# Four column tiles for the K and V matmuls of a low-rank attention decode kernel, with K loaded first

## The chip, the cores and the metric

The kernel runs on one core of a Trainium2 chip. The metric is the device time of one execution in microseconds. Of the kernel before, single runs lie between 656.4 and 669.9 us, so medians and ratios of several runs are compared. Profiles are single executions, and their "span" is up to 6 us shorter than the time of the same run.

## The reference

```python
B, H, Sq, Skv, Dh, R = 2, 16, 1, 8192, 256, 8     # bf16, k and v are 134 MB each
kp = einsum("rn,bhnd->bhrd", e_proj, k)            # 8192 keys are projected to 8
vp = einsum("rn,bhnd->bhrd", f_proj, v)
scores = einsum("bhqd,bhrd->bhqr", q, kp) * Dh ** -0.5
o = einsum("bhqr,bhrd->bhqd", softmax(scores), vp)
```

All of k and v, 268 MB, must be read once. Everything else is small.

## The kernel before

Two heads ("a pair") are handled together in each of 16 iterations. `kt` and `vt` hold a pair's K and V, 8 MB each (64 KB in each partition), and **each has one buffer**. The 8192 keys of a head lie on 64 partitions with 128 columns `j`, so a K group is 64 matmuls of 128x512 and a V group 128 matmuls of 128x256. The stationary operand has only 32 columns in both. V's weights are softmax(scores) times `f_proj`, so V's matmuls give the output rows directly.

```python
FIRST_K = (64, 64); LAST_K = (64, 32, 16, 8, 8); LAST_V = (64, 24, 16, 10, 6, 4, 2, 2)
W_AHEAD = 24
# ... SyncE: loads
nc.sync.dma_start(out=st[:, 0], in_=e_v).then_inc(s_st, 16)      # the projections
nc.sync.dma_start(out=st[:, 1], in_=f_v).then_inc(s_st, 16)
for a in range(NP):                                               # 16 pairs
    if a > 0:
        nc.sync.wait_ge(s_kr, a)            # K's buffer is released by its last matmul
    ...                                     # load kt: whole, or in FIRST_K / LAST_K pieces
    if a > 0:
        nc.sync.wait_ge(s_vr, a)            # V's buffer likewise
    ...                                     # load vt: whole, or in LAST_V pieces
# ... TensorE, one iteration
for j in range(0, J, 2):                    # J = 128
    mm = nc.tensor.matmul(acc_k[:], lhsT=wk[:, j:j + 2, :]..., rhs=kt[:, j:j + 2, :]...,
                          start=(j == 0), stop=(j == J - 2))
mm.then_inc(s_kr, 1)
...                                         # softmax on VectorE and ScalarE
for j in range(J):
    mm = nc.tensor.matmul(o_ps[:], lhsT=wp[:, j, :], rhs=vt[:, j, :], start=False,
                          stop=(j == J - 1), skip_group_check=True)
mm.then_inc(s_vr, 1)
```

(Cuts are marked by `...`; the `wait_ge` on the landing of a load ahead of each group is left out.)

## Time and profile before

| | before |
|---|---|
| median of 3 runs (lowest to highest) | 665.48 us (660.8 to 669.93) |
| profiled run: time, span, granted TensorE clock | 656.35 us, 654.3 us, 0.896 |
| end of the last packet of a load, by the packet records | 640.6 us |

First, lines of the page of the kernel before. "q1" is the queue of the loads; its last number is the share of 16 engines' span that packets were in flight. PE is TensorE, PEld its weight loads, DVE VectorE, ACT ScalarE, POOL GpSimd, and SP SyncE. The granted clock is the share of TensorE's full clock that the throttle let through. Part 5 lines end with busy us, mean ns, then the idle time before the group and who ended it.

```profile
span 654.3 us, 7393 instructions
...
PE 522.7 (80%) x3233; PEld 327.6 (50%) x3233; DVE 98.7 (15%) x280; ACT 16.3 (2%) x36; POOL 8.3 (1%) x12
...
q1 hardware_dynamic: 6720, 268.73, 96.5%
...
HBM read 268.71 MB, written 0.02 MB: 411 GB/s over the span
...
DMA 55%; PE 43%; DVE 1%; issue 1%; SPq 0%; ACT 0%; DVEq 0%; ACTq 0%
...
L213 PE MATMUL o_ps<-vt,wp 128*32 128x256 bf16 x2048 | 258.9, 295 | 40.4 <-DMA vt<-in_v_dram 33.8
L197 PE MATMUL acc_k<-kt,wk 128*32 128x512 bf16 x1024 | 246.0, 405 | 40.7 <-DMA kt<-in_k_dram 40.7
```

TensorE waits 41 us in 14 K groups and 34 us in the V groups, 2 to 3 us each. The next fence is the view of DMA issues of the same kernel: median us from the issue of a whole 8 MB load to its landing.

```profile
vt<-in_v_dram SPq DMA_DIRECT2D x15, 23.6
kt<-in_k_dram SPq DMA_DIRECT2D x14, 24.0
```

A load that is queued in good time lands about 19.4 us after the one before it (see the changed kernel below), so here a load is issued only about 4 us before the load ahead of it has landed. I call this time the **lead**: from the issue of a load to the landing of the one before it.

The end of the execution, from the timeline of TensorE (start us, us, engine, line, operation):

```profile
617.43 13.99 PE L197 MATMUL acc_k<-kt,wk 128*32 128x512 bf16 x64
633.33 0.28 PE L203 MATMUL pb<-p_77,ones_81 1*64 1x8 f32 x4 [1.91 <-ACT p_77 L232]
635.26 15.80 PE L213 MATMUL o_ps<-vt,wp 128*32 128x256 bf16 x128 [1.65 <-DVE wp L279]
```

And in windows (from and to, length, then busy us and instructions of PE, weight loads, DVE, ACT and POOL, then granted clock, DMA share and GB/s), first the steady state, then the tail:

```profile
100.00:600.00 500.00, 404.56 (x2455) 249.42 (x2452) 73.19 (x214) 10.27 (x26) 0.00 (x0) 0.89 0.99 420
```

```profile
620.00:639.00 19.00, 15.44 (x77) 7.87 (x76) 5.83 (x17) 0.21 (x1) 0.00 (x0) 0.91 0.98 412
640.00:651.00 11.00, 11.00 (x102) 9.59 (x99) 0.00 (x0) 0.00 (x0) 0.00 (x0) 1.00 0.01 3
```

After 640 us the DMA is done and TensorE works alone for 11 us. Look also at the steady state: the DMA is "99% busy" at 420 GB/s. That share counts a packet as busy however long it takes. Most packets carry 64 KB and take 2.418 us in the median; sixteen engines at that pace would move 434 GB/s.

Where I quote idle engines and slow packets below, they are my sums over the trace's packet records: *idle* is the time in which fewer than 16 packets were in flight, weighted by the engines that had none and divided by 16; *slow* is the time of 64 KB packets above 2.418 us, divided by 16. Both are then microseconds of the whole DMA.

### The profile page before, as it was taken

Reading aid. Unit: us, or ns where it says so; the run is one execution under the profiler, and the core shown is the slowest. Engines: PE = TensorE matmul, PEld = TensorE weight load, DVE = VectorE, ACT = ScalarE, POOL = GpSimd, SP = SyncE. Lnnn points to the kernel's source line nnn. Section 1 sums busy time; section 2 is a strip of 40 time slices with the busy share of each in tenths; the row PEclk is TensorE's granted clock in tenths of the full one; section 3 lists DMA queues with packets and bytes.
Section 4 is the critical chain, followed back from the end, with each engine's and each line's share of the span. In section 5 each row is a group of like instructions: output and inputs, shape, how many; then the busy total and the mean of one; then the engine's idle time right before and its main releaser. Section 6 shows DMA issues by size and latency. Waiting matters only on the chain.

```text
span 654.3 us, 7393 instructions
## 1 busy us (share of the span) xinstructions
PE 522.7 (80%) x3233; PEld 327.6 (50%) x3233; DVE 98.7 (15%) x280; ACT 16.3 (2%) x36; POOL 8.3 (1%) x12
## 2 busy tenths in 40 slices
PE   4577988777977869868788787769877789687978
PEld 3246374453835528345363644638354373553736
DVE  1030020301103030030300203021030300303030
ACT  0200000000000000000000000000000000000000
POOL 5000000000000000000000000000000000000000
PEclk9689878899877898878999788999887898788999
DMA  9999999999999999999999999999999999999991
GB/s 367 420 437 445 409 437 389 445 437 401 425 421 437 381 445 393 441 389 389 449 449 421 413 445 417 421 449 441 421 421 421 413 433 393 449 393 409 423 414 39
DMA packets 6721, 268.75 MB, mean 411 GB/s; under 512 B 768, under 2 KB 1344, under 8 KB 1984
## 3 DMA queue, kind: packets, MB, share of 16 engines
q1 hardware_dynamic: 6720, 268.73, 96.5%
q8 instruction: 1, 0.02, 0.0%
HBM read 268.71 MB, written 0.02 MB: 411 GB/s over the span
## 4 chain that ended last, share of the span: by engine, by line
DMA 55%; PE 43%; DVE 1%; issue 1%; SPq 0%; ACT 0%; DVEq 0%; ACTq 0%
DMA kt<-in_k_dram 44%; PE acc_k L197 33%; PE o_ps L213 10%; DMA vt<-in_v_dram 7%; DMA q_69<-in_q_dram 3%; DVE prod L256 0%; PE q_ps L187 0%; SPq L137 0%; DVE wtmp L272 0%; DVE wp_83 L276 0%; PE pb L203 0%; ACT o_sb L235 0%; DVE wp L279 0%; ACT p_77 L232 0%; SPq L141 0%
## 5 line engine op out<-in xcount | busy, mean ns | idle before, releaser
L213 PE MATMUL o_ps<-vt,wp 128*32 128x256 bf16 x2048 | 258.9, 295 | 40.4 <-DMA vt<-in_v_dram 33.8
L197 PE MATMUL acc_k<-kt,wk 128*32 128x512 bf16 x1024 | 246.0, 405 | 40.7 <-DMA kt<-in_k_dram 40.7
L213 PEld LDWEIGHTS o_ps<-vt,wp 128*32 128x32 bf16 x2048 | 213.7, 105 | 82.5 <-DMA vt<-in_v_dram 40.0
L197 PEld LDWEIGHTS acc_k<-kt,wk 128*32 128x32 bf16 x1024 | 103.4, 102 | 179.9 <-DMA kt<-in_k_dram 44.6
L256 DVE SCALAR_TENSOR_TENSOR prod<-acc_k,q_sb 32x512 f32<-32x512 f32 x16 | 10.8, 678 | 288.7 <-PE acc_k L197 288.7
L253 DVE MEMSET wp<- x16 | 4.4, 272 | 215.5 <-PE o_ps L213 213.0
L203 PE MATMUL pb<-p_77,ones_81 1*64 1x8 f32 x64 | 4.5, 208 | 30.6 <-ACT p_77 L232 30.6
L272 DVE TENSOR_TENSOR wtmp<-fw,pb 128x192 f32<-128x192 bf16 (+1 forms) x32 | 22.0, 687 | 10.6 <-PE pb L203 10.1
L203 PEld LDWEIGHTS pb<-p_77,ones_81 1*64 1x64 f32 x64 | 3.1, 129 | 38.5 <-ACT p_77 L232 38.5
L276 DVE TENSOR_REDUCE wp_83<-wtmp 128x24 f32<-128x192 f32 (+1 forms) x32 | 22.0, 686 | 1.1
L230 ACT CAST q_sb<-q_ps 32x512 bf16<-32x512 f32 x16 | 9.2, 575 | 297.2 <-PE q_ps L187 297.2
L169 PE MATMUL ps_e<-st,sel 128*128 128x128 bf16 x32 | 6.9, 270 | 9.4 <-POOL sel_q L117 8.4
L232 ACT ACTIVATE p_77<-s_75 1x16 f32<-1x16 f32 x16 | 3.4, 215 | 303.1 <-DVE s_75 L268 303.1
L278 DVE CAST wp<-wp_83 64x24 f32 (+1 forms) x32 | 9.6, 299 | 4.4
L187 PE MATMUL q_ps<-q_69,sel_q 32*32 32x256 bf16 x32 | 6.4, 281 | 4.8 <-DMA q_69<-in_q_dram 4.8
L279 DVE CAST wp<-wp_83 64x24 f32 (+1 forms) x32 | 9.7, 304 | 0.4
L169 PEld LDWEIGHTS ps_e<-st,sel 128*128 x32 | 3.5, 109 | 11.3 <-issue 10.8
L169 PE MATMUL ps_f<-st,sel 128*128 128x128 bf16 x32 | 6.7, 272 | 0.0
L187 PEld LDWEIGHTS q_ps<-q_69,sel_q 32*32 x32 | 1.8, 89 | 8.3 <-issue 8.2
L169 PEld LDWEIGHTS ps_f<-st,sel 128*128 x32 | 3.8, 119 | 0.1
L110 POOL MEMSET sel<- 128x4096 bf16 x1 | 3.5, 3512 | 0.5 <-SPq L98 0.5
L260 DVE STREAM_TRANSPOSE sc_out<-sc_in 32x32 f32<-32x32 f32 x16 | 3.2, 199 | 0.5
(27 smaller groups left out, 27.6 us busy)
## 6 DMA issues: line engine op xcount, KB each, us to landing
kt<-in_k_dram SPq DMA_DIRECT2D x3, 4096.0 KB, 14.1
vt<-in_v_dram SPq DMA_DIRECT2D x1, 4096.0 KB, 13.8
kt<-in_k_dram SPq DMA_DIRECT2D x1, 2048.0 KB, 18.7
vt<-in_v_dram SPq DMA_DIRECT2D x1, 1536.0 KB, 17.1
kt<-in_k_dram SPq DMA_DIRECT2D x1, 1024.0 KB, 20.7
kt<-in_k_dram SPq DMA_DIRECT2D x2, 512.0 KB, 22.1
vt<-in_v_dram SPq DMA_DIRECT2D x1, 1024.0 KB, 19.1
vt<-in_v_dram SPq DMA_DIRECT2D x1, 640.0 KB, 20.2
```

The lines of the kernel that those rows point to most:

```text
L169: mm = nc.tensor.matmul(ps[:, bass.ds(r, 1), :].rearrange("p o j -> p (o j)"), lhsT=pick, rhs=st[:, i, x, :], start=(x == 0), stop=(x == X ...
L187: mm = nc.tensor.matmul(q_ps[:, b * Dh:(b + 1) * Dh], lhsT=sel_q[:, bass.ds(it, 1), b, :].rearrange("k a m -> k (a m)"), rhs=q16[:], start ...
L197: mm = nc.tensor.matmul(acc_k[:], lhsT=wk[:, j:j + 2, :].rearrange("p j m -> p (j m)"), rhs=kt[:, j:j + 2, :].rearrange("p j d -> p (j d)" ...
L203: mm = nc.tensor.matmul(pb[g * PH:(g + 1) * PH, :], lhsT=ones1[:], rhs=p16[:, g, :], start=True, stop=True)
L213: mm = nc.tensor.matmul(o_ps[:], lhsT=wp[:, j, :], rhs=vt[:, j, :], start=False, stop=(j == J - 1), skip_group_check=True)
L230: nc.scalar.copy(out=q_sb[:], in_=q_ps[:]).then_inc(s_qa, 1)
L253: nc.vector.memset(wp[:, :, bass.ds(old, G)], 0.0)
L256: then(0, nc.vector.scalar_tensor_tensor(out=prod[:], in0=acc_k[:], scalar=scale, in1=q_sb[:], op0=ALU.mult, op1=ALU.mult, accum_out=sc_in ...
L272: then(4 + i, nc.vector.tensor_tensor(out=wtmp[:, lo:hi], in0=fw[:, lo:hi], in1=pb[:].unsqueeze(1).to_broadcast([P, hi - lo, R]), op=ALU.m ...
L276: then(6 + i, nc.vector.reduce_sum(out=wp32[:, lo:hi], in_=wtmp[:, lo:hi], axis=AX.X))
L278: nc.vector.tensor_copy(out=wp[0:PH, lo:hi, bass.ds(col, 1)], in_=wp32[0:PH, lo:hi].unsqueeze(2))
L279: then(0, nc.vector.tensor_copy(out=wp[PH:P, lo:hi, bass.ds(col + 1, 1)], in_=wp32[PH:P, lo:hi].unsqueeze(2)), (s_wa, s_wb)[i])
```

## The change

The intent: the stationary operand has 32 columns, so three quarters of the TensorE array stand idle. K's matmuls go round four column tiles (four sets of 32 output partitions), and so do V's first 96; V's four partial sums are added by an fp32 matmul with a selection matrix (`fsel`) half way through the last 32 columns, which use two tiles, one for each half of the 256 output columns. The softmax is done on all 128 partitions at once, loads are whole 8 MB transfers except for V's last, and K's first load is issued ahead of the projections.

```diff
-FIRST_K = (64, 64)
-LAST_K = (64, 32, 16, 8, 8)
-LAST_V = (64, 24, 16, 10, 6, 4, 2, 2)
-W_AHEAD = 24
+LAST_V = (64, 32, 16, 10, 4, 2)
+SPREAD = 96
+FOLD = 112
 ...
-        nc.sync.dma_start(out=st[:, 0], in_=e_v).then_inc(s_st, 16)
-        nc.sync.dma_start(out=st[:, 1], in_=f_v).then_inc(s_st, 16)
         for a in range(NP):
             if a > 0:
                 nc.sync.wait_ge(s_kr, a)
+            nc.sync.dma_start(out=kt[:], in_=k_t[a]).then_inc(s_kd, 16)
             if a == 0:
-                load(kt, k_t[a], FIRST_K, s_kf)
+                nc.sync.dma_start(out=st[:, 0], in_=e_v).then_inc(s_st, 16)
+                nc.sync.dma_start(out=st[:, 1], in_=f_v).then_inc(s_st, 16)
 ...
-            for j in range(0, J, 2):
-                mm = nc.tensor.matmul(acc_k[:], ..., start=(j == 0), stop=(j == J - 2))
+            for i in range(J // 2):
+                mm = nc.tensor.matmul(tile4(acc_k, i % CT), ...,
+                                      start=(i < CT), stop=(i >= J // 2 - CT), skip_group_check=True)
             mm.then_inc(s_kr, 1)
 ...
             for j in range(J):
-                mm = nc.tensor.matmul(o_ps[:], lhsT=wp[:, j, :], rhs=vt[:, j, :], ...)
+                if j == FOLD:
+                    nc.tensor.wait_ge(s_ev, t1)
+                    for x in range(X):
+                        nc.tensor.matmul(tile4(o_x, x)[:, 0:DX], lhsT=fsel[:], rhs=o4_sb[:, x * DX:(x + 1) * DX], ...)
+                if j < SPREAD:
+                    mm = nc.tensor.matmul(tile4(o_4, j % CT)[:, 0:Dh], lhsT=wp[:, j, :], rhs=vt[:, j, :],
+                                          start=(j < CT), stop=(j >= SPREAD - CT), skip_group_check=True)
+                else:
+                    for x in range(X):
+                        mm = nc.tensor.matmul(tile4(o_x, x)[:, 0:DX], lhsT=wp[:, j, :],
+                                              rhs=vt[:, j, x * DX:(x + 1) * DX], ...)
             mm.then_inc(s_vr, 1)
```

(Cut: waits, semaphores, the constants, the loads of the later pairs, and the softmax, which sums by one fp32 matmul with a mask in place of a transpose. With `W_AHEAD` goes the early start of V: its matmuls began when the weights of the first 24 columns were ready, and now wait for all of them.)

More of the change, by code (lines that the diff above doesn't have):

```diff
@@ L46 @@
     GR = G * R
+    CT = 4
+    W = P // CT
+    X = 2
+    DX = Dh // X
     C = P // R
     XB = PH // C
-    assert Sq == 1 and BH == 32 and J == 128 and 2 * GR == 32 and C * XB == PH
-    assert sum(FIRST_K) == J and sum(LAST_K) == J and sum(LAST_V) == J
+    assert Sq == 1 and BH == W and J == 128 and 2 * GR == W and C * XB == PH
+    assert sum(LAST_V) == J and SPREAD % CT == 0
     scale = float(Dh) ** -0.5
-    TQ = 32
     sb = ctx.enter_context(tc.tile_pool(name="sb", bufs=1))
@@ L65 @@
     q16 = sb.tile([BH, Dh], BF16, name="q16")
-    sel_q = sb.tile([BH, NP, 2, GR * 2], BF16, name="sel_q")
-    q_sb = sb.tile([2 * GR, 2 * Dh], BF16, name="q_sb")
-    prod = sb.tile([2 * GR, 2 * Dh], FP32, name="prod")
-    sc_in = sb.tile([TQ, TQ], FP32, name="sc_in")
-    sc_out = sb.tile([TQ, TQ], FP32, name="sc_out")
-    s16 = sb.tile([1, G, R], FP32, name="s16")
-    nmax = sb.tile([1, G], FP32, name="nmax")
-    p16 = sb.tile([1, G, R], FP32, name="p16")
-    ssum = sb.tile([1, G], FP32, name="ssum")
-    rs_in = sb.tile([TQ, TQ], FP32, name="rs_in")
-    rs_out = sb.tile([TQ, TQ], FP32, name="rs_out")
-    ones1 = sb.tile([1, PH], FP32, name="ones1")
+    sel_q = sb.tile([BH, NP, 2, CT, 2, GR], BF16, name="sel_q")
+    q_sb = sb.tile([P, 2 * Dh], BF16, name="q_sb")
+    ident = sb.tile([P, P], FP32, name="ident")
+    sel_r = sb.tile([P, R], FP32, name="sel_r")
+    sel_g = sb.tile([P, G], FP32, name="sel_g")
+    gmask = sb.tile([P, G, PH], FP32, name="gmask")
+    fsel = sb.tile([P, W], FP32, name="fsel")
+    prod = sb.tile([P, 2 * Dh], FP32, name="prod")
+    sc = sb.tile([P, 1], FP32, name="sc")
+    scr = sb.tile([P, R], FP32, name="scr")
+    nmax = sb.tile([P, 1], FP32, name="nmax")
+    p32 = sb.tile([P, R], FP32, name="p32")
+    ssum = sb.tile([P, 1], FP32, name="ssum")
+    rs = sb.tile([P, 1], FP32, name="rs")
     wtmp = sb.tile([P, J, R], FP32, name="wtmp")
     wp32 = sb.tile([P, J], FP32, name="wp32")
+    o4_sb = sb.tile([P, Dh], FP32, name="o4_sb")
     o_sb = sb.tile([BH, Dh], BF16, name="o_sb")
@@ L83 @@
     ps_f = pp.tile([P, R, J], FP32, name="ps_f")
-    acc_k = pp.tile([2 * GR, 2 * Dh], FP32, name="acc_k")
-    o_ps = pp.tile([BH, Dh], FP32, name="o_ps")
-    q_ps = pp.tile([2 * GR, 2 * Dh], FP32, name="q_ps")
-    pb = pp.tile([P, R], FP32, name="pb")
+    acc_k = pp.tile([P, 2 * Dh], FP32, name="acc_k")
+    o_4 = pp.tile([P, 2 * Dh], FP32, name="o_4")
+    o_x = pp.tile([P, 4 * DX], FP32, name="o_x")
+    q_ps = pp.tile([P, 2 * Dh], FP32, name="q_ps")
+    s_ps = ps_e[:].rearrange("p r j -> p (r j)")[:, 0:R]
     k_t = k.rearrange("b h (p j) d -> (b h p) j d", p=PH).rearrange("(a q) j d -> a q j d", q=P)
@@ L94 @@
     f_v = f_proj.rearrange("r (c x j) -> (r c) x j", c=C, x=XB)
-    starts = lambda parts: {sum(parts[:i]): i for i in range(len(parts))}
+    last_v = {sum(LAST_V[:i]): i for i in range(len(LAST_V))}
     with tc.tile_critical(name="main"):
@@ L100 @@
         s_st, s_qd, s_out, s_kd, s_vd, s_kr, s_vr = (sem(n) for n in ("st", "qd", "out", "kd", "vd", "kr", "vr"))
-        s_kf = [sem(f"kf{i}") for i in range(len(FIRST_K))]
-        s_kl = [sem(f"kl{i}") for i in range(len(LAST_K))]
         s_vl = [sem(f"vl{i}") for i in range(len(LAST_V))]
-        s_zi, s_cst, s_wk, s_e, s_f, s_w0, s_f0 = (sem(n) for n in ("zi", "cst", "wk", "e", "f", "w0", "f0"))
-        s_q, s_qa, s_x, s_ex, s_pb, s_wa, s_wb = (sem(n) for n in ("q", "qa", "x", "ex", "pb", "wa", "wb"))
-        s_d = [sem(f"d{i}") for i in range(9)]
-        s_rs, s_fin = sem("rs"), sem("fin")
+        s_zi, s_id, s_cst, s_wk, s_e, s_f, s_w0, s_f0 = (
+            sem(n) for n in ("zi", "id", "cst", "wk", "e", "f", "w0", "f0"))
+        s_q, s_qa, s_sc, s_sp, s_mx, s_ex, s_w, s_o4, s_ev, s_fin = (
+            sem(n) for n in ("q", "qa", "sc", "sp", "mx", "ex", "w", "o4", "ev", "fin"))
+        s_d = [sem(f"d{i}") for i in range(8)]
         nc.gpsimd.memset(sel[:], 0.0).then_inc(s_zi, 1)
-        nc.gpsimd.wait_ge(s_zi, 1)
+        nc.gpsimd.memset(sel_q[:], 0.0).then_inc(s_zi, 1)
+        nc.gpsimd.memset(ident[:], 0.0).then_inc(s_zi, 1)
+        nc.gpsimd.wait_ge(s_zi, 3)
         for x in range(XB):
@@ L116 @@
             ).then_inc(s_zi, 1)
-        nc.gpsimd.memset(sel_q[:], 0.0).then_inc(s_zi, 1)
-        nc.gpsimd.wait_ge(s_zi, 2 + XB)
+        nc.gpsimd.affine_select(
+            out=ident[:], in_=ident[:], compare_op=ALU.not_equal, fill=1.0,
+            base=0, pattern=[[-1, P]], channel_multiplier=1,
+        ).then_inc(s_id, 1)
         for b in range(2):
-            nc.gpsimd.affine_select(
-                out=sel_q[:, :, b, b * GR:(b + 1) * GR], in_=sel_q[:, :, b, b * GR:(b + 1) * GR],
-                compare_op=ALU.not_equal, fill=1.0,
-                base=0, pattern=[[-G, NP], [-1, G], [0, R]], channel_multiplier=1,
-            ).then_inc(s_cst, 1)
+            for c in range(CT):
+                sl = sel_q[:, :, b, c, b].rearrange("k a (g r) -> k a g r", g=G)
+                nc.gpsimd.affine_select(
+                    out=sl, in_=sl, compare_op=ALU.not_equal, fill=1.0,
+                    base=0, pattern=[[-G, NP], [-1, G], [0, R]], channel_multiplier=1,
+                ).then_inc(s_cst, 1)
@@ L125 @@
         nc.vector.memset(wk[:], 0.0).then_inc(s_wk, 1)
-        nc.vector.memset(wp[:], 0.0).then_inc(s_cst, 1)
         nc.vector.memset(z0[:], 0.0)
-        nc.vector.memset(sc_in[:], 0.0)
-        nc.vector.memset(rs_in[:], 0.0)
-        nc.vector.memset(ones1[:], 1.0).then_inc(s_cst, 1)
-        NCST = 4
-        def load(dst, src, parts, sems):
-            j0 = 0
-            for js, s in zip(parts, sems, strict=True):
-                nc.sync.dma_start(out=dst[:, j0:j0 + js, :], in_=src[:, j0:j0 + js, :]).then_inc(s, 16)
-                j0 += js
@@ L140 @@
-        nc.sync.dma_start(out=st[:, 0], in_=e_v).then_inc(s_st, 16)
-        nc.sync.dma_start(out=st[:, 1], in_=f_v).then_inc(s_st, 16)
+        nc.vector.memset(wp[:], 0.0)
+        nc.vector.wait_ge(s_id, 1)
+        nc.vector.reduce_sum(out=sel_r[:], in_=ident[:].rearrange("k (i r) -> k r i", r=R), axis=AX.X)
+        nc.vector.reduce_sum(out=sel_g[:], in_=ident[:].rearrange("k (i g r) -> k g i r", g=G, r=R),
+                             axis=AX.XY).then_inc(s_id, 1)
+        nc.vector.reduce_sum(out=fsel[:], in_=ident[:].rearrange("k (c m) -> k m c", c=CT), axis=AX.X)
@@ L142 @@
+        nc.vector.wait_ge(s_id, 2)
+        nc.vector.tensor_copy(out=gmask[:],
+                              in_=sel_g[:].unsqueeze(2).to_broadcast([P, G, PH])).then_inc(s_cst, 1)
+        NCST = 2 * CT + 1
         for a in range(NP):
@@ L144 @@
                 nc.sync.wait_ge(s_kr, a)
+            nc.sync.dma_start(out=kt[:], in_=k_t[a]).then_inc(s_kd, 16)
             if a == 0:
-                load(kt, k_t[a], FIRST_K, s_kf)
+                nc.sync.dma_start(out=st[:, 0], in_=e_v).then_inc(s_st, 16)
+                nc.sync.dma_start(out=st[:, 1], in_=f_v).then_inc(s_st, 16)
                 nc.sync.dma_start(out=q16[:], in_=q_v).then_inc(s_qd, 16)
-            elif a < NP - 1:
-                load(kt, k_t[a], (J,), (s_kd,))
-            else:
-                load(kt, k_t[a], LAST_K, s_kl)
             if a > 0:
@@ L154, with tile4 @@
             if a < NP - 1:
-                load(vt, v_t[a], (J,), (s_vd,))
+                nc.sync.dma_start(out=vt[:], in_=v_t[a]).then_inc(s_vd, 16)
             else:
-                load(vt, v_t[a], LAST_V, s_vl)
-        nc.sync.wait_ge(s_fin, 1)
+                j0 = 0
+                for js, s in zip(LAST_V, s_vl, strict=True):
+                    nc.sync.dma_start(out=vt[:, j0:j0 + js], in_=v_t[a][:, j0:j0 + js]).then_inc(s, 16)
+                    j0 += js
+        nc.sync.wait_ge(s_fin, X)
         nc.sync.dma_start(out=o_v, in_=o_sb[:]).then_inc(s_out, 16)
         nc.sync.wait_ge(s_out, 16)
-        nc.tensor.wait_ge(s_zi, 2 + XB)
+        def tile4(ps, c):
+            return ps[c * W:(c + 1) * W]
+        nc.tensor.wait_ge(s_zi, 3 + XB)
         nc.tensor.wait_ge(s_st, 32)
@@ L174 @@
         nc.tensor.wait_ge(s_w0, 2)
-        nc.tensor.matmul(o_ps[:], lhsT=z0[:],
-                         rhs=wk[:, 0:Dh // GR, :].rearrange("p j m -> p (j m)"), start=True, stop=False,
-                         skip_group_check=True)
+        for x in range(X):
+            nc.tensor.matmul(tile4(o_x, x)[:, 0:DX], lhsT=z0[:],
+                             rhs=wk[:, 0:DX // GR, :].rearrange("p j m -> p (j m)"), start=True, stop=False,
+                             skip_group_check=True)
         nc.tensor.wait_ge(s_qd, 16)
-        first_k, last_k, last_v = starts(FIRST_K), starts(LAST_K), starts(LAST_V)
         with nc.tensor.Fori(0, NP) as it:
@@ L183 @@
             last = nc.tensor.snap((it // (NP - 1)) * 16)
+            tk = nc.tensor.snap((it + 1) * 16)
             tv = nc.tensor.snap((it + 1) * 16 - last)
-            tk = nc.tensor.snap(it * 16 - last)
             for b in range(2):
                 mm = nc.tensor.matmul(q_ps[:, b * Dh:(b + 1) * Dh],
-                                      lhsT=sel_q[:, bass.ds(it, 1), b, :].rearrange("k a m -> k (a m)"), rhs=q16[:],
-                                      start=True, stop=True)
+                                      lhsT=sel_q[:, bass.ds(it, 1), b].rearrange("k a c b m -> k (a c b m)"),
+                                      rhs=q16[:], start=True, stop=True)
@@ L190 @@
             mm.then_inc(s_q, 1)
             nc.tensor.wait_ge(s_kd, tk)
-            for j in range(0, J, 2):
-                if j in first_k:
-                    nc.tensor.wait_ge(s_kf[first_k[j]], 16)
-                if j in last_k:
-                    nc.tensor.wait_ge(s_kl[last_k[j]], last)
-                mm = nc.tensor.matmul(acc_k[:], lhsT=wk[:, j:j + 2, :].rearrange("p j m -> p (j m)"),
-                                      rhs=kt[:, j:j + 2, :].rearrange("p j d -> p (j d)"),
-                                      start=(j == 0), stop=(j == J - 2))
@@ L200 @@
-            mm.then_inc(s_kr, 1)
-            nc.tensor.wait_ge(s_ex, t1)
-            for g in range(G):
-                mm = nc.tensor.matmul(pb[g * PH:(g + 1) * PH, :], lhsT=ones1[:], rhs=p16[:, g, :],
-                                      start=True, stop=True)
-            mm.then_inc(s_pb, 1)
-            nc.tensor.wait_ge(s_wa, t1)
+            for i in range(J // 2):
+                mm = nc.tensor.matmul(tile4(acc_k, i % CT), lhsT=wk[:, 2 * i:2 * i + 2].rearrange("p j m -> p (j m)"),
+                                      rhs=kt[:, 2 * i:2 * i + 2].rearrange("p j d -> p (j d)"),
+                                      start=(i < CT), stop=(i >= J // 2 - CT), skip_group_check=True)
@@ L207 @@
+            mm.then_inc(s_kr, 1)
+            nc.tensor.wait_ge(s_sc, t1)
+            nc.tensor.matmul(s_ps, lhsT=gmask[:].rearrange("k g p -> k (g p)"), rhs=scr[:],
+                             start=True, stop=True).then_inc(s_sp, 1)
+            nc.tensor.wait_ge(s_w, t1)
             nc.tensor.wait_ge(s_vd, tv)
             for j in range(J):
-                if j == W_AHEAD:
-                    nc.tensor.wait_ge(s_wb, t1)
                 if j in last_v:
                     nc.tensor.wait_ge(s_vl[last_v[j]], last)
-                mm = nc.tensor.matmul(o_ps[:], lhsT=wp[:, j, :], rhs=vt[:, j, :], start=False,
-                                      stop=(j == J - 1), skip_group_check=True)
+                if j == FOLD:
+                    nc.tensor.wait_ge(s_ev, t1)
+                    for x in range(X):
+                        nc.tensor.matmul(tile4(o_x, x)[:, 0:DX], lhsT=fsel[:], rhs=o4_sb[:, x * DX:(x + 1) * DX],
+                                         start=False, stop=False, skip_group_check=True)
+                if j < SPREAD:
+                    mm = nc.tensor.matmul(tile4(o_4, j % CT)[:, 0:Dh], lhsT=wp[:, j, :], rhs=vt[:, j, :],
+                                          start=(j < CT), stop=(j >= SPREAD - CT), skip_group_check=True)
+                    if j == SPREAD - 1:
+                        mm.then_inc(s_o4, 1)
+                else:
+                    for x in range(X):
+                        mm = nc.tensor.matmul(tile4(o_x, x)[:, 0:DX], lhsT=wp[:, j, :],
+                                              rhs=vt[:, j, x * DX:(x + 1) * DX], start=False,
+                                              stop=(j == J - 1), skip_group_check=True)
@@ L230 @@
             nc.scalar.copy(out=q_sb[:], in_=q_ps[:]).then_inc(s_qa, 1)
-            nc.scalar.wait_ge(s_x, t1)
-            nc.scalar.activation(out=p16[:], in_=s16[:], func=ACT.Exp).then_inc(s_ex, 1)
-        nc.scalar.wait_ge(s_rs, NP + 1)
+            nc.scalar.wait_ge(s_mx, t1)
+            nc.scalar.activation(out=p32[:], in_=s_ps, func=ACT.Exp, bias=nmax[:], accum_out=ssum[:]).then_inc(s_ex, 1)
+            nc.scalar.wait_ge(s_o4, t1)
+            nc.scalar.copy(out=o4_sb[:], in_=o_4[:, 0:Dh]).then_inc(s_ev, 1)
         nc.scalar.wait_ge(s_vr, NP)
-        nc.scalar.mul(o_sb[:], o_ps[:], rs_out[:, 0:1]).then_inc(s_fin, 1)
+        nc.scalar.copy(out=o_sb[:, 0:DX], in_=o_x[0:BH, 0:DX]).then_inc(s_fin, 1)
         nc.vector.wait_ge(s_wk, 1)
@@ L240 @@
         nc.vector.tensor_copy(out=wk[PH:P, :, R:GR], in_=ps_e[PH:P].rearrange("p r j -> p j r")).then_inc(s_w0, 1)
-        nc.vector.wait_ge(s_cst, NCST)
         nc.vector.wait_ge(s_f0, 1)
@@ L247 @@
             old = nc.vector.snap((it * G + (BH - G)) % BH)
-            def then(i, inst, s=None):
-                inst.then_inc(s_d[i] if s is None else s, 1)
             nc.vector.wait_ge(s_vr, t0)
@@ L255 @@
             nc.vector.wait_ge(s_kr, t1)
-            then(0, nc.vector.scalar_tensor_tensor(out=prod[:], in0=acc_k[:], scalar=scale, in1=q_sb[:],
-                                                   op0=ALU.mult, op1=ALU.mult,
-                                                   accum_out=sc_in[0:2 * GR, 0:1]))
+            nc.vector.scalar_tensor_tensor(out=prod[:], in0=acc_k[:], scalar=scale, in1=q_sb[:],
+                                           op0=ALU.mult, op1=ALU.mult, accum_out=sc[:]).then_inc(s_d[0], 1)
@@ L259 @@
             nc.vector.wait_ge(s_d[0], t1)
-            then(1, nc.vector.transpose(out=sc_out[:], in_=sc_in[:]))
+            nc.vector.tensor_scalar(out=scr[:], in0=sel_r[:], scalar1=sc[:], scalar2=None,
+                                    op0=ALU.mult).then_inc(s_sc, 1)
+            nc.vector.wait_ge(s_sp, t1)
+            nc.vector.reduce_max(out=nmax[:], in_=s_ps, axis=AX.X, negate=True).then_inc(s_mx, 1)
+            nc.vector.wait_ge(s_ex, t1)
+            nc.vector.tensor_tensor(out=wtmp[:], in0=fw[:], in1=p32[:].unsqueeze(1).to_broadcast([P, J, R]),
+                                    op=ALU.mult).then_inc(s_d[1], 1)
@@ L261 @@
+            nc.vector.reciprocal(out=rs[:], in_=ssum[:]).then_inc(s_d[2], 1)
             nc.vector.wait_ge(s_d[1], t1)
-            then(2, nc.vector.tensor_tensor(
-                out=s16[:].rearrange("o g r -> o (g r)"), in0=sc_out[0:1, 0:GR], in1=sc_out[0:1, GR:2 * GR],
-                op=ALU.add))
+            nc.vector.reduce_sum(out=wp32[:], in_=wtmp[:], axis=AX.X).then_inc(s_d[3], 1)
             nc.vector.wait_ge(s_d[2], t1)
-            then(3, nc.vector.reduce_max(out=nmax[:], in_=s16[:], axis=AX.X, negate=True))
@@ L267 @@
             nc.vector.wait_ge(s_d[3], t1)
-            then(0, nc.vector.tensor_tensor(out=s16[:], in0=s16[:],
-                                            in1=nmax[:].unsqueeze(2).to_broadcast([1, G, R]), op=ALU.add), s_x)
-            nc.vector.wait_ge(s_pb, t1)
-            for i, (lo, hi) in enumerate(((0, W_AHEAD), (W_AHEAD, J))):
-                then(4 + i, nc.vector.tensor_tensor(
-                    out=wtmp[:, lo:hi], in0=fw[:, lo:hi],
-                    in1=pb[:].unsqueeze(1).to_broadcast([P, hi - lo, R]), op=ALU.mult))
-                nc.vector.wait_ge(s_d[4 + i], t1)
-                then(6 + i, nc.vector.reduce_sum(out=wp32[:, lo:hi], in_=wtmp[:, lo:hi], axis=AX.X))
-                nc.vector.wait_ge(s_d[6 + i], t1)
-                nc.vector.tensor_copy(out=wp[0:PH, lo:hi, bass.ds(col, 1)], in_=wp32[0:PH, lo:hi].unsqueeze(2))
-                then(0, nc.vector.tensor_copy(out=wp[PH:P, lo:hi, bass.ds(col + 1, 1)],
-                                              in_=wp32[PH:P, lo:hi].unsqueeze(2)), (s_wa, s_wb)[i])
@@ L281 @@
-            then(8, nc.vector.reduce_sum(out=ssum[:], in_=p16[:], axis=AX.X))
-            nc.vector.wait_ge(s_d[8], t1)
-            nc.vector.reciprocal(out=rs_in[0:1, bass.ds(col, G)], in_=ssum[:]).then_inc(s_rs, 1)
-        nc.vector.wait_ge(s_rs, NP)
-        nc.vector.transpose(out=rs_out[:], in_=rs_in[:]).then_inc(s_rs, 1)
+            nc.vector.tensor_scalar(out=wp[0:PH, :, bass.ds(col, 1)], in0=wp32[0:PH].unsqueeze(2),
+                                    scalar1=rs[0:PH], scalar2=None, op0=ALU.mult)
@@ L289 @@
+            nc.vector.tensor_scalar(out=wp[PH:P, :, bass.ds(col + 1, 1)], in0=wp32[PH:P].unsqueeze(2),
+                                    scalar1=rs[PH:P], scalar2=None, op0=ALU.mult).then_inc(s_w, 1)
+        nc.vector.wait_ge(s_vr, NP)
+        nc.vector.tensor_copy(out=o_sb[:, DX:Dh], in_=o_x[BH:2 * BH, 0:DX]).then_inc(s_fin, 1)
 _INS = ['q', 'k', 'v', 'e_proj', 'f_proj']
```

## The prediction

> **What bounds the kernel now.** The DMA stream: the page gives the queue 96.5% of 16 engines' span, TensorE 80%. Most DMA packets of the trace carry 64 KB, median 2.418 us; sixteen engines at that pace move 434 GB/s, the fabric ceiling (435 GB/s) of the Trainium skill, "DMA: Bandwidth & Descriptors", Specifications, so the trace agrees. The change moves the same bytes.
>
> What lies outside that floor, in the profiled run (span 654.3):
> - Tail. In narrow windows the DMA share falls to nothing at about 639.6 us, but PE works to 651.1 (timeline): the last K group (64 matmuls, 13.9 us) starts only at 617.5, the softmax takes 3.8, and 128 V matmuls 15.8. Then output copy and store, 3.2 us.
> - Gaps between transfers. A pair takes about 39.6 us of DMA and 36.8 of PE (15.5 K, 3.9 softmax, 16.8 V, 0.6 rest). Each buffer is single: a load is issued only when the buffer's matmuls end, V's only 2.3 to 4.5 us before the running K load lands (the waits; mean about 2.6). Issue to first packet took about 1.1 us at the start, and the engines do not finish together, so some run dry. By the packet records, fewer than 16 engines are active in about fifteen short stretches, worth 7 us of all engines.
> - Slow 64 KB packets (over 2.418 us), about 9 us. I expect no change here.
>
> **What the change does.**
> - K: 64 matmuls in four column tiles. The skill, "TensorE: Matmul & The Clock Gate", Part 3, reports 2.38x for 3 column tiles; no run here shows it yet. Estimate from this trace: 15.5 us (216 ns each warm, a cold start on top) becomes 5 to 7. V: 16.8 becomes 6 to 8, with the fold. PE's clock will start each burst low; that costs nothing under the DMA.
> - Softmax: different operations, 3.5 to 4.5 us, hidden under V's load.
> - Steady state: each load is issued 12 to 15 us before the running one ends; the engines never run dry: up to 7 us back.
> - Tail: only the last V pieces are left after the stream, about 1 us of PE, then 3.2 us. About 11 us back.
> - Start: K first puts the 256 KB of projections behind 8 MB, landing at about 24 us instead of 3. Building the weights took 11.1 us (8.4 to 19.5). K's matmuls start at about 36 us rather than 25 and end at 41; V's load keeps the DMA busy to about 43. A bubble of 0 to 2 us.
> - Fewer small pieces: below 1 us.
>
> Net in the profiled state: 654.3 - 11 - 7 + 1, about 637. Unprofiled runs were slower before (660.8 to 669.9), which I cannot attribute; I take the same 17.5 us from the median: 648.
>
> **What would show it.** PE below 45%, K's group at or under 7 us; PE's waits on DMA 10 us or more per group; DMA at 98% or more of the span; the chain of waits over 90% DMA; the end within 5 us of the last load's packet; no DMA gap except perhaps near 42 us.
>
> **What would make it wrong.** Column tiles that do not overlap: K stays at 15 us, the tail stays, and a hole of 8 us opens at the start. Tiles reading four moving streams that slow the DMA's writes: longer 64 KB packets during PE bursts. More slow packets than assumed. If gaps in the unprofiled runs exceed the profiled one's, the gain is larger, to 638.
>
> Predicted 648 us, 637 to 657; faster by over 2% 0.66, within 2% 0.32, slower 0.02.

## The result, and the profile after

| | before | after |
|---|---|---|
| median of 4 runs | 663.93 us | 632.23 us |
| lowest to highest | 660.8 to 669.93 | 631.76 to 633.09 |
| profiled span | 654.3 us | 630.0 us |
| end of the last packet of a load | 640.6 us | 626.1 us |

(The profiled run of before, 656.35 us, is not among these four; that of the changed kernel, 631.76 us, is.) The ratio is 0.951, 95% interval 0.944 to 0.959. A ratio is the mean time of one kernel's fast runs over that of the other's of the same rounds, so not quite the ratio of the medians. The direction was right, the gain was larger than the range allowed: 632.2 us lies below 637.

The same lines of the page, of the changed kernel:

```profile
span 630.0 us, 8346 instructions
...
PE 223.6 (35%) x3778; PEld 139.7 (22%) x3778; DVE 83.1 (13%) x169; ACT 24.6 (4%) x68; POOL 14.8 (2%) x20
...
q1 hardware_dynamic: 5712, 268.73, 98.9%
...
HBM read 268.71 MB, written 0.02 MB: 427 GB/s over the span
...
DMA 78%; PE 19%; issue 1%; DVE 1%; SPq 0%; ACT 0%; DVEq 0%; ACTq 0%
...
L206 PE MATMUL acc_k<-kt,wk 128*32 128x512 bf16 x1024 | 92.0, 538 | 178.0 <-DMA kt<-in_k_dram 178.0
L224 PE MATMUL o_91<-vt,wp 128*32 128x256 bf16 x1536 | 78.3, 396 | 177.7 <-DMA vt<-in_v_dram 168.3
```

TensorE now waits 12 us ahead of each group. (The mean of one K matmul rose from 405 to 538 ns while the group's busy time fell from 246 to 92 us: four run at a time. The mean of an overlapped matmul is no cost.) The issues and the end of the timeline:

```profile
kt<-in_k_dram SPq DMA_DIRECT2D x16, 32.7
...
vt<-in_v_dram SPq DMA_DIRECT2D x15, 31.7
```

```profile
606.96 5.22 PE L206 MATMUL acc_k<-kt,wk 128*32 128x512 bf16 x64 [11.54 <-DMA kt<-in_k_dram]
613.33 0.39 PE L211 MATMUL ps_e<-scr,gmask 128*128 128x8 f32 x2 [1.15 <-DVE scr L273]
618.39 5.31 PE L224 MATMUL o_91<-vt,wp 128*32 128x256 bf16 x96 [4.68 <-DVE wp L287]
624.05 1.07 PE L230 MATMUL o_x<-vt,wp 128*32 128x128 bf16 x32 [0.34 <-DMA vt<-in_v_dram]
625.62 0.41 PE L221 MATMUL o_x<-o_sb,fsel 128*32 128x128 f32 x4 [0.50 <-DMA vt<-in_v_dram]
625.87 1.06 PE L230 MATMUL o_x<-vt,wp 128*32 128x128 bf16 x32
```

And the steady state in a window:

```profile
100.00:600.00 500.00, 175.37 (x3016) 108.17 (x3016) 63.04 (x130) 17.16 (x52) 0.00 (x0) 0.65 1.00 432
```

A K group takes 4.9 to 6.5 us instead of 14.0 to 16.7. A whole load is now 32 us from issue to landing, and that is *good*: it was issued 12 to 14 us before the load ahead of it landed, and queued. The DMA share went only from 0.99 to 1.00, but the rate from 420 to 432 GB/s. Between the last packet of a load and the end there are 3.9 us (630.0 less 626.1), where there were 13.7.

The 24.3 us between the two spans, by place:

| | before | after | gain |
|---|---|---|---|
| idle engines at load boundaries | 7.2 us | 0.8 us | 6.4 |
| slow packets at load boundaries | 8.5 us | 0.9 us | 7.6 |
| rest of the stream (not measured apart; fewer small pieces, rounding) | | | 0.5 |
| tail: last packet of a load to end of span | 13.7 us | 3.9 us | 9.8 |

The second line is the one that the prediction had at zero.

### The profile page after: what moved, and what is told of

Read it like the earlier page. It is cut to its first block, busy times and chain, and to the rows that moved or that the text cites. A ratio compares the mean times of both kernels' runs of the same rounds, so it can differ in the third digit from the quotient of the medians.

```text
span 630.0 us, 8346 instructions
## 1 busy us (share of the span) xinstructions
PE 223.6 (35%) x3778; PEld 139.7 (22%) x3778; DVE 83.1 (13%) x169; ACT 24.6 (4%) x68; POOL 14.8 (2%) x20
## 3 DMA queue, kind: packets, MB, share of 16 engines
q1 hardware_dynamic: 5712, 268.73, 98.9%
## 4 chain that ended last, share of the span: by engine, by line
DMA 78%; PE 19%; issue 1%; DVE 1%; SPq 0%; ACT 0%; DVEq 0%; ACTq 0%
DMA vt<-in_v_dram 75%; PE o_91 L224 12%; PE o_x L230 5%; DMA st<-in_f_proj_dram 3%; PE acc_k L206 1%; PE ps_e L182 1%; PE o_x L221 1%; PE ps_f L182 0%; DVE wtmp L278 0%; SPq L166 0%; DVE wp_85 L282 0%; ACT wk L242 0%; DVE prod L270 0%; PE q_ps L200 0%; DVE wp L287 0%
## 5 line engine op out<-in xcount | busy, mean ns | idle before, releaser
L206 PE MATMUL acc_k<-kt,wk 128*32 128x512 bf16 x1024 | 92.0, 538 | 178.0 <-DMA kt<-in_k_dram 178.0
L224 PE MATMUL o_91<-vt,wp 128*32 128x256 bf16 x1536 | 78.3, 396 | 177.7 <-DMA vt<-in_v_dram 168.3
L224 PEld LDWEIGHTS o_91<-vt,wp 128*32 128x32 bf16 x1536 | 57.3, 140 | 194.4 <-DMA vt<-in_v_dram 169.6
L206 PEld LDWEIGHTS acc_k<-kt,wk 128*32 128x32 bf16 x1024 | 34.1, 130 | 231.3 <-DMA kt<-in_k_dram 181.0
L270 DVE SCALAR_TENSOR_TENSOR prod<-acc_k,q_sb 128x512 f32<-128x512 f32 x16 | 11.1, 692 | 267.8 <-PE acc_k L206 267.8
L230 PE MATMUL o_x<-vt,wp 128*32 128x128 bf16 x1024 | 35.6, 224 | 1.1 <-issue 0.8
L230 PEld LDWEIGHTS o_x<-vt,wp 128*32 128x32 bf16 x1024 | 33.1, 100 | 2.6 <-issue 1.0
L278 DVE TENSOR_TENSOR wtmp<-fw,p_81 128x1024 f32<-128x1024 bf16 x16 | 19.6, 1225 | 6.8 <-ACT p_81 L250 6.8
L282 DVE TENSOR_REDUCE wp_85<-wtmp 128x128 f32<-128x1024 f32 x16 | 19.5, 1220 | 0.0
L285 DVE TENSOR_SCALAR wp<-wp_85,rs 64x128 f32 x16 | 8.0, 497 | 3.4 <-DVE wp_85 L282 3.4
L287 DVE TENSOR_SCALAR wp<-wp_85,rs 64x128 f32 x16 | 8.1, 504 | 0.2
```

Source lines behind the costliest of these rows:

```text
L206: mm = nc.tensor.matmul(tile4(acc_k, i % CT), lhsT=wk[:, 2 * i:2 * i + 2].rearrange("p j m -> p (j m)"), rhs=kt[:, 2 * i:2 * i + 2].rearra ...
L224: mm = nc.tensor.matmul(tile4(o_4, j % CT)[:, 0:Dh], lhsT=wp[:, j, :], rhs=vt[:, j, :], start=(j < CT), stop=(j >= SPREAD - CT), skip_grou ...
L230: mm = nc.tensor.matmul(tile4(o_x, x)[:, 0:DX], lhsT=wp[:, j, :], rhs=vt[:, j, x * DX:(x + 1) * DX], start=False, stop=(j == J - 1), skip_ ...
L270: nc.vector.scalar_tensor_tensor(out=prod[:], in0=acc_k[:], scalar=scale, in1=q_sb[:], op0=ALU.mult, op1=ALU.mult, accum_out=sc[:]).then_i ...
L278: nc.vector.tensor_tensor(out=wtmp[:], in0=fw[:], in1=p32[:].unsqueeze(1).to_broadcast([P, J, R]), op=ALU.mult).then_inc(s_d[1], 1)
L282: nc.vector.reduce_sum(out=wp32[:], in_=wtmp[:], axis=AX.X).then_inc(s_d[3], 1)
```

## The experiments

Two theories of the slow packets were open after the result. **Restart theory**: they and the idle engines are both the price of an engine that ran dry, because the next load was issued too late; the first packets after a restart take about 3 us instead of 2.42. The slow packets of the trace of before speak for it: 214 of the 218 above 2.6 us lie at a boundary between two loads or at the start. **Contention theory**: TensorE at 80% reads SBUF so much that the DMA's writes are slowed, and the boundaries are only where matmuls happen to run too. The two make opposite claims about TensorE's work and about the time of the issue, so each was changed without the other.

### Early issue without column tiles

The kernel before, its matmuls untouched. Each load is split in two halves, and the first half is issued as soon as the matmuls have read that half of the buffer:

```diff
-                nc.sync.wait_ge(s_kr, a)
+                nc.sync.wait_ge(s_krh, a)            # the first 32 K matmuls are done
-                load(kt, k_t[a], (J,), (s_kd,))
+                nc.sync.dma_start(out=kt[:, 0:J // 2], in_=k_t[a][:, 0:J // 2]).then_inc(s_kd, 16)
+                nc.sync.wait_ge(s_kr, a)
+                nc.sync.dma_start(out=kt[:, J // 2:J], in_=k_t[a][:, J // 2:J]).then_inc(s_kd2, 16)
 ...                                                  # V, and the last pair's pieces, likewise
```

> The kernel before, its matmuls untouched, but every load is split in two halves and the first half is issued as soon as the matmuls have read that half of the buffer, about 8 us earlier. Restart theory (the slow packets and the idle engines are both the price of engines that ran dry, so an earlier issue removes both): no gaps but the tail, 64 KB or 32 KB packets all near their median, idle plus slow packets (7 + 8 us in the trace of before) gone, so a span near 640 us and runs that no longer spread over 9 us. Contention theory (PE at 80% slows the DMA's writes into SBUF): the idle 7 us may go, but about 8 us of slow packets stay, span about 648 us.

Measured: 645.5 us, ratio to before 0.972 (0.967 to 0.978). Its steady-state window, with TensorE as busy as before:

```profile
100.00:600.00 500.00, 411.03 (x2523) 256.07 (x2524) 76.50 (x220) 9.68 (x25) 0.00 (x0) 0.90 1.00 431
```

The rate is that of the changed kernel, and the last packet of a load ends at 626.7 us instead of 640.6. The halves travel in packets of 32 KB (median 1.218 us); of 7936 only 19 take over 1.3 us, 18 of them at the start. So about half of the change's gain (17 of 32 us by the medians) needs no column tiles at all, only an earlier issue. TensorE was 82% busy in that window, which speaks against contention. But the smaller packets are a second change in this experiment; the ones below keep 64 KB. What is left is the tail, now 16 us, and the 642.7 us of its span were foretold as 640. Runs still spread over 5.6 us (641.0 to 646.6), which the theory said would not be: it was too strong there.

### TensorE kept busy in the changed kernel

The other way round: the changed kernel with dummy matmuls (512 columns, from a small constant tile) after each release, so the issues stay early while TensorE is busy.

```diff
             mm.then_inc(s_kr, 1)
+            for _ in range(30):
+                nc.tensor.matmul(ps_f..., lhsT=z0[:], rhs=wk[:, 0:32]..., start=True, stop=True, ...)
 ...
             mm.then_inc(s_vr, 1)
+            for _ in range(50):
+                ...                                  # the same
```

> The changed kernel with 30 dummy matmuls (512 columns) after each K group has released its buffer and 50 after each V group, so PE is again near 80% busy and reads SBUF, while every load is issued as early as before. Restart theory: within 2 us of the changed kernel, 632 us. Contention theory: slow packets come back and 6 to 10 us with them, 638 to 642 us.

Measured: 645.3 us, neither. The fault was the experiment's: its last 50 dummies ran from 629.4 to 640.3 us, though the output had been stored at 631.3, and the program waits for them. The steady state was at 432 GB/s, and the slow packets unchanged (2.5 us of the whole DMA, 2.4 in the changed kernel). So it was mended: the dummies stand in loops that shrink to 10 in the last pair.

> The busy experiment mended: the first one let its last 50 dummy matmuls run after the output, 11 us that have nothing to do with the DMA. Now the dummies run in loops that shrink to 10 in the last pair. Restart theory: 632 to 634 us (about 1 us for the last softmax, which starts later), last load packet at the same time as in the changed kernel (about 625 us). Contention theory: 638 to 642 us.

Measured: 632.5 us (631.9 to 634.9). Steady state:

```profile
100.00:600.00 500.00, 376.19 (x4053) 200.90 (x4052) 63.04 (x130) 17.15 (x52) 0.00 (x0) 0.86 1.00 433
```

TensorE is busy for 75% of the window, 376 us instead of 175, and the rate in the window does not fall. Against 632.2 us of the changed kernel, contention of this kind is ruled out: the dummies read a small constant tile, while in the experiment before the real matmuls read K and V. The profiled run was the slowest of the four (634.9 us). Its trace has two gaps, at 43 and 66 us, with 2.7 us of idle engines and leads of -0.2 and 3.0 us; so there, too, cost goes with a short lead.

These dummies gave a number by the way. With the granted clock at 1.00 the 64 K matmuls in four tiles took 3.64 us (here from the first of the two runs with dummies), against 13.99 in one tile at clock 1.00 in the kernel before: 3.8 times faster.

```profile
104.36 3.64 PE L207 MATMUL acc_k<-kt,wk 128*32 128x512 bf16 x64
```

In the changed kernel the last K group takes 5.2 us: its granted clock is 0.50 in the first 2 us and 0.69 over the whole group.

### Late issue in the changed kernel

TensorE as idle as in the changed kernel, but each load is issued later: POOL fills a one-row scratch tile three times between the release and the issue.

```diff
-                nc.sync.wait_ge(s_kr, a)
+                nc.sync.wait_ge(s_pk, a)             # POOL, about 11 us after s_kr
 ...                                                  # V likewise
+                for i in range(3):
+                    nc.gpsimd.memset(idle[:, i], 0.0).then_inc(s_pm, 1)
```

> The changed kernel, PE as little busy as in it, but each load is issued about 11 us later (POOL fills a one-row scratch tile three times between the release and the issue), so that some 1.5 to 2.5 us of the running load are left instead of 12 to 14. Restart theory: gaps at nearly every load, each with idle engines and with first packets of about 3 us, together 0.7 to 1.5 us per load, so 20 to 40 us more: 650 to 672 us. Contention theory: idle time may come, but the packets stay at 2.42 us because PE is at 35%.

Measured: 685.3 us. It is longer than I expected because the delay also counts once at the start (a hole of 12 us ahead of the second K load) and once in the tail; I had only summed the gaps. The steady state answers the question:

```profile
100.00:600.00 500.00, 163.16 (x2902) 102.67 (x2894) 128.66 (x121) 16.79 (x50) 268.87 (x75) 0.66 0.97 412
```

412 GB/s with TensorE 33% busy, and 301 packets of 64 KB above 2.6 us, more than the 218 of the kernel before. At a gap some 14 of the first packets take about 3 us, mostly 0.5 to 0.8 us of the whole DMA, whatever the length of the gap. Why they take longer is not shown. Nor is it quite shown that an engine must have run dry first: at four boundaries of all the traces slow packets of 0.5 to 0.7 us come with next to no idle time in the records. POOL's writing could be blamed, so a shorter delay, about 8 us, came later:

> The changed kernel with each load issued about 8 us later instead of 11: leads of 4 to 5.5 us remain. In all traces so far idle engines and slow packets come with leads under about 3.5 us and vanish above 5. So steady gaps should nearly be gone (under 3 us idle plus slow from the second pair on), leaving the hole of 8 to 9 us at the start and the later last load at the end, 4 to 8 us: 644 to 650 us. If it is not the lead but POOL's writing that made the delayed run slow, it is above 665 like the first.

Measured: 650.5 us, just above the 644 to 650 expected.

```profile
100.00:600.00 500.00, 169.51 (x2908) 103.64 (x2906) 100.40 (x130) 16.76 (x51) 206.16 (x78) 0.66 1.00 432
```

POOL still fills for 206 of 500 us in the window, and the rate is 432 GB/s. So it is not POOL that slows the DMA; the lead does.

### One part of the change at a time

V in four tiles and K in one, then K in four and V in one (its first 120 matmuls). The unused partitions of the accumulator are set to zero once.

```diff
-                mm = nc.tensor.matmul(tile4(acc_k, i % CT), ...
+                mm = nc.tensor.matmul(tile4(acc_k, 0), ...           # K plain
```

```diff
-SPREAD = 96
-FOLD = 112
+SPREAD = 120
+FOLD = 124
-                    mm = nc.tensor.matmul(tile4(o_4, j % CT)[:, 0:Dh], ...
+                    mm = nc.tensor.matmul(tile4(o_4, 0)[:, 0:Dh], ...  # V plain
```

> The changed kernel with all K matmuls in one column tile (V stays in four). K takes 14 to 15.5 us again. Its load then still has about 4 us of lead, so few or no gaps in the steady state; but a hole of about 8 us opens at the start (K's first group starts at 36 us because the weights come late) and the tail grows by about 8 us: 645 to 649 us. If the column tiles of K are what keeps the stream full, gaps come back at every K load, and it is above 655.

> The changed kernel with V's first 120 matmuls in one column tile (K stays in four; fold at 124). V takes about 16.5 us again, so V's load is issued only 2 to 3 us before the K load lands, as in the kernel before. Restart theory: the gaps come back at V's issues alone, with slow packets at each, 10 to 20 us, and the tail grows by about 5 us: 647 to 657 us. If V's column tiles did not matter for the stream, only the tail grows: about 638 us.

Measured: 658.8 us with K plain (0.996 of before, so nearly the whole gain is gone) and 646.1 us with V plain. K's result missed what I expected by 10 us, and V's lies just under the 647 to 657 of the restart theory. The K groups with K plain:

```profile
L209 PE MATMUL acc_k<-kt,wk 128*32 128x512 bf16 x1024 | 260.3, 422 | 144.1 <-DMA kt<-in_k_dram 144.1
```

A K group takes 16.3 us in the mean, longer than the 15.4 before the change; TensorE has waited about 10 us ahead of each, and in the group that starts at 153.2 us, for one, the granted clock is 0.50 for the first 3.8 us. So leads of K are 2.5 to 4 us, and gaps came back at 7 of its 14 later boundaries and at none of V's. The hole at the start is over 10 us and the tail 10 us longer. With V plain, the restarts after the first K load are at V's loads alone, where leads are 2 to 3.6 us. Each group's tiles protect the load that is issued at its end, and K's carry more, since the first K group and the last pair's softmax wait behind them.

### The lead against its cost

The leads differ from load to load, so eleven of the fourteen traces give a curve. For every boundary between two loads (pieces of the last ones left out, and the holes at the start of three runs), by lead:

| lead | boundaries | mean idle + slow, us of the whole DMA |
|---|---|---|
| under 2.5 us | 36 | 1.52 |
| 2.5 to 3.5 us | 54 | 0.83 |
| 3.5 to 5 us | 62 | 0.24 |
| over 5 us | 174 | 0.01 |

The means hide much: between 2.5 and 3.5 us single boundaries cost from 0.02 to 3.0 us, and one of those over 5 us cost 0.7 (a lead of 5.1). The kernel before had a median lead of about 4 us and 11 of 30 below 3.5. The changed kernel has 12 to 14.

### The kernel before, once more

The profiled run of before was one of its fastest, and the prediction could not say why others took longer.

> The kernel before, unchanged, for a second trace: the one at hand (span 654.3) was faster than nearly all other runs of it. If the slower runs are the same gaps, only more or longer, this trace has a span of 656 to 663 us, a tail like the first one's (11 to 12 us of PE after the last load), and more idle engine time than 7 us plus more slow packets than 8 us; packets away from gaps stay at 2.42 us. If the memory itself is slower in those runs, packets are slower everywhere.

Measured: 661.0 us, span 659.0 (a single run, so its state is unknown). Idle engines at boundaries are 7.1 us as in the first trace, but slow packets 11.9 us instead of 8.5: 3.4 of the 4.7 us. From the last packet of a load to the end it is 13.6 us, as in the first trace; the other 1.3 us are not placed. So the slower run has more slow restarts (306 of its 310 slow packets lie at boundaries or at the start), not slower memory. Over the 29 fast runs of before that were made beside the experiments, a lower granted clock goes with a longer span (correlation -0.70; clocks 0.868 to 0.899, spans 651.0 to 662.6). Less clock would mean longer groups and shorter leads, so 1.1 us of TensorE work was added to each V group:

```diff
+            for _ in range(10):
+                mm = nc.tensor.matmul(ps_f..., lhsT=z0[:], rhs=wk[:, 0:Dh // GR]..., start=True, stop=True, ...)
             mm.then_inc(s_vr, 1)
```

> The kernel before with 10 dummy matmuls (256 columns) ahead of each release of V's buffer, about 1.1 us more of PE in each of the 16 pairs, to see why its own runs spread with the granted clock (over 11 runs a clock lower by 0.02 goes with 8 us more; those 0.02 are some 12 us of PE time). If the kernel sits on the edge where each us of PE takes a us of lead and the stream pays for it, about 0.7 us for each us: 10 to 18 us more, 672 to 680 us. If it is bound by the DMA with slack on PE (36.8 of 39.6 us per pair, as I read it in the prediction), at most 3 us more.

Measured: 667.9 us, ratio 1.007 (1.001 to 1.014). Inconclusive: slower by 5 us, between the two expectations, and the interval only just excludes no change. Idle engines rose to 12.1 us and slow packets to 10.3 us, as the restart theory has it, yet the granted clock rose too (0.89 to 0.91), so the addition was partly paid back. Why the clock differs from run to run stays open, and with it the full spread of the kernel before. One run of before in these rounds took 1790 us at clock 1.00; it counts as slow and is left out.

### The projections first again

```diff
+        nc.sync.dma_start(out=st[:, 0], in_=e_v).then_inc(s_st, 16)   # ahead of the loop
+        nc.sync.dma_start(out=st[:, 1], in_=f_v).then_inc(s_st, 16)
         for a in range(NP):
 ...
             if a == 0:
-                nc.sync.dma_start(out=st[:, 0], in_=e_v).then_inc(s_st, 16)
-                nc.sync.dma_start(out=st[:, 1], in_=f_v).then_inc(s_st, 16)
```

> The changed kernel with the projections loaded first again, as in the kernel before (this part of the change undone). The gap at 42 to 43.6 us (0.7 us idle, 0.6 us slow packets) should go, and nothing else change: about 1.3 us less than the changed kernel, 630.9 us. If K first had been worth anything, it would be slower.

Measured: 630.7 us (630.6 to 631.2), 0.952 of before (0.949 to 0.956). The gap at 42 us is gone, and the span is 628.7 instead of 630.0. So "K first" gains nothing, and may cost about a microsecond. Last, with the fold ahead of the wait for a late piece as well, beside an unchanged run:

> The changed kernel, unchanged, on the same chip and in the same rounds as the candidate below, and for a second trace: 632 us, runs within 1.5 us of each other, one gap near 42 us costing some 1.3 us and none after it.

> The changed kernel with the projections loaded first (as measured before, 630.7 us) and, besides, the fold of V's four partial sums placed ahead of the wait for the load piece that begins at column 112, where PE waited 0.5 us in the last pair. The start gives 1.3 to 1.5 us and the fold up to 0.4 us: 630.3 us. If the fold is hidden in any case, 630.7 us.

Measured in the same rounds: 631.2 us for the changed kernel (0.950 of before) and 630.7 us for the candidate (0.950). The difference of the spans, 629.2 against 628.6, is smaller than foretold because this time the changed kernel's gap near 42 us was only 0.1 us idle and 0.7 us slow. The fold's place is worth nothing that these runs could show. With the projections first the profiled spans were 0.6 to 1.3 us shorter than the changed kernel's, but the times of these last eight runs overlap (630.4 to 631.9 against 630.9 to 631.8). What it gains is at the edge of what these runs can tell.

## Why the prediction was wrong

- **"Slow 64 KB packets (over 2.418 us), about 9 us. I expect no change here."** This is the step that failed. The count was right (8.5 us of it at boundaries), the cause was not looked for. They were the second half of the price of a short lead, and they fell to 0.9 us. Those 7.6 us are about the whole of the 7 us by which the profiled run (630.0) beat my 637 for that state. A look at *when* these packets ran, 214 of 218 at a boundary or at the start, would have pointed to it before the change.
- **"I take the same 17.5 us from the median."** The second mis-sized term. The profiled run of before was 9.1 us faster than the median of the three runs I had; of the changed kernel it lies 0.5 us below the median. I carried the 9.1 us over into the changed kernel, where they are not. The second trace of before shows part of why: 3.4 of its 4.7 us more are slow packets at boundaries, which the change removes; for the rest of the spread the cause stays open. My last sentence allowed for it ("the gain is larger, to 638"), but by too little. The first term (7 us) and this one (about 9) make up the 16 us between 648 and 632.2.
- **Gaps, up to 7 us**: right; 6.4 us were gained.
- **Tail, about 11 us**: nearly right; 9.8 us.
- **Softmax, 3.5 to 4.5 us**: wrong. From the end of the last K group to the start of V it takes 6.2 us (612.2 to 618.4), where it took 3.8 before. It cost nothing here, since the last piece of V lands only at 626.5.
- **K 5 to 7 us, V 6 to 8**: right, 4.9 to 6.5 and, but for the first and last pair (8.7 and 8.5), 6.1 to 7.6. The Trainium skill, "TensorE: Matmul & The Clock Gate", Part 3, has 2.38x for three tiles, which is 0.79 for each tile; the 3.8x measured here for four at full clock is 0.96 for each, so more than the page would lead one to expect. The same page, Part 1, says that the clock falls after some 3.4 us without matmuls; here TensorE waits 12 us ahead of a group, the last K group starts at a granted clock of 0.50, and the mean fell from 0.896 to 0.675. Under the DMA it cost nothing, as predicted.
- **A bubble of 0 to 2 us near 42 us**: right; 0.74 us idle and 0.59 us slow, and 0.1 and 0.7 in a second trace.
- **What would show it**: PE below 45% (35%), waits of 10 us or more per group (12), DMA share 98% or more (98.9%), the end within 5 us of the last load's packet (3.9) all came. "The chain of waits over 90% DMA" did not: it says 78%, since the chain goes through the V matmuls that release the buffer before each load, although they no longer set the pace.
- The slack was read too kindly: "39.6 us of DMA and 36.8 of PE" compares sums, but with one buffer each, a load can't be issued while its buffer is read, and what counted was how long before the end of the running load that moment came.

## What to carry to other kernels

With one buffer for each stream, look at the lead, the time from a load's issue to the landing of the one before it: here, leads over 5 us cost next to nothing and leads of 2.5 to 3.5 us cost 0.8 us each in the mean. In the kernel before, half of this cost lay in packets that count as busy. A DMA share of 99% therefore proves little; compare the rate with what the median packet would give. To buy lead, shorten the work that holds the buffer, or release it in halves, which here gave the same rate without touching a matmul.

## What the Trainium skill lacked or had wrong

- "DMA: Bandwidth & Descriptors", Rules for kernel authors, says to issue a DMA early so that its fixed cost overlaps, but not how early. Here leads over 5 us cost next to nothing (174 boundaries, 0.01 us each in the mean) and leads under 2.5 us cost 1.5 us each.
- The same page does not have the slow restart: at a boundary with too short a lead, some 14 of the first 64 KB packets took about 3 us instead of 2.42. No page has it.
- The same page, Specifications, gives 435 GB/s as the fabric ceiling; the median packet agrees (434 GB/s), and a stream with enough lead held 432 to 434 GB/s for 500 us. "HBM Reference", Specifications (TRN2), says about 425 GB/s for a core that streams alone; that is below what these windows show.
- "TensorE: Matmul & The Clock Gate", Part 3, has a measured speedup for three column tiles and none for four, nor has any other page: here 13.99 us against 3.64 us for the same 64 matmuls, 3.8 times.
- "Perfetto Trace Analysis", Identifying the Most-Contended Engine, says to take HBM utilization for the DMA, which these runs bear out, and gives the reason that there are 16 engines; these runs show a second one: the share of time in which packets are in flight counts slow ones as busy, 0.99 at 420 GB/s and 1.00 at 432 GB/s.
